# One core, one transformer layer: the value weights issued by SyncE, five warming products, another written-out order

## The chip, the cores and the metric

The kernel runs on one core of a Trainium2 chip. A core has five engines with a queue each: TensorE (PE in the profile; its weight loads are PEld), VectorE (DVE), ScalarE (ACT), GpSimd (POOL) and SyncE (SP), which here only issues DMAs. An engine takes its own queue strictly in order and waits on semaphores that the others raise. The metric is the device time of one execution in microseconds (us), before and after.

## The reference

`x` is 2048 x 448, in bf16. The layer is a linear attention with 16 heads of 28 columns, followed by a gated feed-forward of width 1792, each behind a layernorm and with a residual:

```python
qkv = (layernorm(x) @ wqkv) split into q, k, v of 16 heads
phi(q) = concat(softmax(q @ w_phi), softmax(-(q @ w_phi)))      # the same for k
kv = sum over s of phi(k)^T v ;  z = sum over s of phi(k)
o = (phi(q) @ kv) / (phi(q) . z + 1e-6)
h = x + o @ wo
h2 = h + (sigmoid(layernorm(h) @ w_gate) * (layernorm(h) @ w_up)) @ w_down
```

## The kernel before

**Tiles.** The 2048 rows are 16 tiles of 128 rows, numbered t = 0 to 15. Everything is a list of named tasks, one or a few instructions each, with an engine, a duration that the planner assumed, a latency (`lat`), dependencies and PSUM banks. `PLAN` (lines 30 to 71) writes out by number the order in which all tasks are put into the five queues; `planned()` (L113) reads it and `emit()` (L147) puts a semaphore wait ahead of a task where it needs one. A number followed by a point names the PSUM banks; a number followed by `~` puts the task on its other engine (`alt`). The durations and latencies in the text are what the planner worked with when it wrote the order: they issue nothing themselves.

**Start.** The q and k weights are multiplied with the per-head matrices `w_phi` first. `WT` (L431, PE) transposes a block of `wq` or `wk`, `mW` and `WTc` (L439, L446) centre it and copy it out, `PhiK` (L420, POOL) spreads `w_phi` into block diagonals, `fold` (L461, PE) multiplies, and `W2` (L469 on ACT, L472 on DVE) copies the product into `Wk2` or `Wq2`. The value weights `Wv` are centred only: `csum` (L477, PE) sums their columns, `csb` (L483, ACT) scales that and `Wvc` (L486, DVE) adds it. The first two tiles of x are transposed on PE (`xP`, L538, copied out by `xTc`, L544), the others by transposing DMAs (`xT0`, `xT1`, L349). `wm` (L413) are three products of constants into a bank nobody reads, which keep PE at work before data arrives; `dm` (L787) are spare products of the same kind which the plan places where it wants, five in all.

**Attention, keys and values.** For each pair of tiles: `kp` and `vp` (L500, PE) project, each in two halves, of which the second must follow the first. The statistics of x are `bst`, `agg` (L519, L521, DVE) and `ve`, `pow`, `neg` (L527 to L531, POOL). `ekp` and `ekm` (L572, ACT) are the two exponentials, `v1` (L577, ACT) the scaled values, `ss` and `rs` (L585, L588, DVE) sums and reciprocals, `phi` (L592, POOL at 1.7 us, or DVE at 1.1 us) the normalization, and `kv` (L605, PE) adds the tile's outer product to bank 4. There are three buffers each for the exponentials, `phi` and `v1`. DVE and POOL are kept from running large SBUF operations at once: a `phi` or `em` on DVE waits for the POOL task ahead of it in the plan, and the next POOL task waits for it (L126 to L133).

**Attention, queries.** `qp` (L500) projects, `eqp` and `eqm` (L627, ACT) exponentiate, `hs` (L641, POOL), `sq` (L637, L644, DVE), `rq0` (L646, DVE), `rq` (L648, POOL) and `em` (L654, POOL or DVE) normalize, and `eT` (L662) is a transposing DMA. When `kv` of tile 15 is done, `kvz` (L669, DVE) takes the sum out of PSUM. Then, by tile: `num` (L678, PE), `rd` and `o` (L686, L688, DVE), a transpose of o (`oP`, L696 on PE, for tiles 0 and 1; the DMA `oT`, L709, for pairs from tile 2), `wo_` (L723, L500), the residual `h` and its statistics `bst2`, `agg2` (L728, L745, L747), `ve2`, `pow2`, `nb` (L748 to L761, POOL), the normalized `hn` (L757, L763), and its transpose `hT` (`hP`, L771 on PE and a copy for tiles 0 and 1; a DMA, L783, after that).

**Feed-forward.** The tiles go in five chunks of 2, 4, 4, 4 and 2. `gu` (L500 with `wg_sb` and `wu_sb`) makes gate and up products for one chunk, seven groups per chunk, once `hT` of all of its tiles is there; `tg` (L818, ACT) is the tanh, `hh` (L825, DVE) the product, `dn` (L844, PE) the down product, `fin` (L851, DVE) the residual, `st` (L853, SP) the store.

**Loads.** SP issues, in the plan's order, `wk0 wk1 phk x0 x2 xT0(2) xT1(2) x4 xT0(4) wo1 xT1(4) wq0 wq1 x8` and so on (`x4` is tiles 4 to 7 of x). The two loads of the value weights, `wv0` and `wv1`, 224 KB each, are issued by ACT, behind `actld` (L336), an exponential of one column of `warm` that loads the table. At the very end `emit()` makes SP wait for all 44 DMA semaphores, in the order of their rings (L191 to L193):

```python
            for k, n in rings.items():
                for i in range(min(n, nring[k])):
                    wait("sp", ring_sems[k][i], (k, i), 16 * ((nring[k] - 1 - i) // n + 1))
```

Of the kernel before, what the change touches and what calls it, by code (L numbers as in the profile page):

```python
# [10 lines left out]
P = 128  # L11
# [19 lines left out]
20 14 18 3 19 21 11 2 8 9 12 0 23 24 16 43 7 17 5 57.7-7 58 59 653.0-0 68.0-0 69 15 10 1 6 62.1-1 63 65.2-2 66  # L31
71.3-3 25 26 22 29 27 28 30 31 32 70 64 67 72 73 116 118 4 654.0-0 655.0-0 163.4-4 164 60 61 165.5-5 89.6-6 92.7-7
86.0-0 95.1-1 93 96 90 87 166 91 88 117 119 94~ 120 121 122 97~ 656.2-2 110.2-2 111 125 123 113 126 124 112 132 130
134 136 131 135 133 137 167.3-5 127 128 44 129 114 138 33 46 34 35 36 37 38 39 40 41 45 42 47 139 168 172 185.6-7
179 171 186 187.0-1 169.2-3 188 170 178 189 190 191 180 173 174 175 74.4-4 181 176 75 76 77.5-5 80.6-6 203.0-3
177.4-4 182 78 192 141 193 81 79 197 196 198 140 183 199 194 115 145 200 204 207 208 205.2-5 221.1-7 206 83.0-0 184
195 222 82 214 215 209 216 210 143 211 217 84 218 201 226 225 212 85 219 223.3-6 101.2-2 224 107.5-5 202 213 108 102
239.0-1 240 232 233 103 234 109 227 144 142 147 228 148 146 149 13 150 151 243 244 235 229 156 158 236 152 246 157
159 154 247 155 153 230 237 241.2-7 220 104.6-6 105 242 98.5-5 99 257.0-3 258 231 245 100 251 106 250 262 311.2-5
238 248~ 160 161 162 249 253 254 255 252 261 268 264 265 266 312 277.1-6 275.0-7 269 314 313 319 271 272 273 276 315  # L40
280 279 320 259.2-3 260 278 256 263 267 293.0-5 282 283 284 287 286 270 281 294 289 290 321 316 322 291 297 305 298
327.2-7 295.1-3 288 304 274 328 337 296 299 285 330 306 336 345.0-6 362.1-5 346 329 363 292 355 354 347 372 348 371
364 323 317 324 300 307 301 308 318 302~ 303 309~ 310 51 49 55 56 48 50 52 326 325 54 447 338 331 339 356 379.3-7
453.2-2 380 448.6-6 511.4-4 454 332 455 340 449 333 657.0-0 456.0-0 349 357 450 350 430.2-5 341 334 358 351 342 335
359 352 382 457 389 381 365 512 513 451.0-0 452 431 507.6-6 508 440 388 514 344 343 360~ 535 353~ 536 361 509 529
413.1-3 396.0-7 461.4-4 414 433 432 510 439 423 366 530 367 537 531 368 462 538 539.2-2 532 458.6-6 463 459 533.5-5
460 397 369 373 374 370 375 540 534 416 415 422 693.2-4 694.5-6 695 696 697 699 376 377 465.1-1 468.3-3 698 383 390
700 469 466 470 701.2-4 702.5-6 703 704 406 405 399 398 707 705 464 53 515.3-7 516 384 467 385 391 708 706 392 549
541 709.0-1 710.5-6 711 712 713 715 717.2-4 718.3-7 719 720 378 714 550 542 475.0-0 472.1-1 716 543 721 723 471
517.5-6 518 722 473 551 476 474 477 557 565 724 386 387 393 394 400 544 545 546 552 407 553 554 395 725.2-4 726.0-1  # L50
727 728 733.5-6 734.3-7 735 736 558 547 729 731 555 559 730 732 566 560 561 562 741.2-4 742.0-1 743 744 739 737 563
478 548 567 740 738 745 747 568 569 570 519.3-7 401 746 748 482.5-5 479.6-6 752.2-2 520 483 480 481 402 408 424 417
425 484 426 418 403 571 556 564 572 755.0-1 756.4-6 757 758 404 409 427 410 573 581 441 411 753 582 574 583 584 585
434 761 759 762 760 435 763.3-5 764.2-7 765 766 767 769 771.4-6 772.0-1 773 774 768 442 419 420 770 777 775 428~ 778
# [11 lines left out]
938 888.3-3 885.5-5 889 886 879.2-2 880 946 882.4-4 944 883 644 751 652 890 959.3-5 960.0-2 961 962 963 965 966 964
967.1-6 968.4-7 969 970 973 971 975.0-2 976.3-5 977 978 972 974 981 979 982 980 983.1-6 984.4-7 985 986 987 989 988
990 991.3-5 992.0-2 993 994 999.1-6 1000.4-7 1001 1002 997 995 996 998 1007.3-5 1008.0-2 1009 1010 1003 1005 1004
1013 1014 1006 1023.1-1 956.6-6 957 1011 950.0-0 1012 951 953.2-2 1027.4-4 1024 954 881 822 884 952 955 887 958
1019.7-7 947.6-6 948 949 1028 1029 1025 1026 1020 1021 1022 1030 1015.3-3 1016 1017 1018  # L70
# [8 lines left out]
class _Graph:  # L79
# [33 lines left out]
    def planned(self):  # L113
# [3 lines left out]
        for item in PLAN.split():  # L117
# [29 lines left out]
    def emit(self, rings):  # L147
# [4 lines left out]
        with ExitStack() as es:  # L152
# [56 lines left out]
def build(nc, A_x, A_wqkv, A_w_phi, A_wo, B_w_gate, B_w_up, B_w_down, out):  # L209
# [16 lines left out]
    with ExitStack() as es:  # L226
# [667 lines left out]
```

## Time and profile before

| | us |
|---|---|
| runs of before | 206.13, 207.4, 208.04 (median 207.4) |
| the profiled execution: its time | 207.14 |
| the profiled execution: its span | 205.4 |
| PE busy | 196.1 (95%) |
| DVE busy | 131.2 (64%) |
| ACT busy | 97.5 (47%) |
| POOL busy | 77.2 (38%) |
| DMA, mean of the core's 16 engines | 103 GB/s |

The span is from the first to the last instruction; the execution's own time is 1.7 us longer. Times in the traces count from the span's start. PE's share is of modelled ends of pipelined products, so that 95% doesn't mean that it works at its best rate. The second part of the page shows the span in 40 slices of 5.1 us, in tenths:

```profile
PE   5999999997989799999999999999999999999994
DVE  2699999896979797886654387553664324352213
ACT  3869999999996461232531003374245130242000
POOL 8459997976787754803600002310003000000000
DMA  4999999219499973430565700054001200100022
```

Four engines are full in the first eight slices, the keys and values; from slice 16 on PE alone is.

### The profile page before, as it was taken

The numbers are of one execution on the slowest core, as the hardware profiler recorded it, in microseconds if no ns is written. First come the engines' busy times: TensorE is split into PE (matmuls) and PEld (weight loads), VectorE is DVE, ScalarE is ACT, GpSimd is POOL, SyncE is SP. The second block draws the span as 40 slices with busy tenths as digits, with TensorE's granted clock in tenths as the row PEclk, the third lists the DMA queues.
The fourth block names the chain that finished last, engine by engine and source line by source line (L and its number), as shares of the span: only waits on it lengthen the run. The fifth ranks groups of instructions, "written<-read, shape, count | busy, mean of one in ns | idle before, by whom it ended". The sixth has DMA issues, their size and how long they took to land.

```text
span 205.4 us, 5009 instructions
## 1 busy us (share of the span) xinstructions
PE 196.1 (95%) x2032; PEld 108.0 (53%) x2033; DVE 131.2 (64%) x304; ACT 97.5 (47%) x186; POOL 77.2 (38%) x139
## 2 busy tenths in 40 slices
PE   5999999997989799999999999999999999999994
PEld 2544544453456584555555554444444445786573
DVE  2699999896979797886654387553664324352213
ACT  3869999999996461232531003374245130242000
POOL 8459997976787754803600002310003000000000
PEclk9999999999999999999999999999999999999999
DMA  4999999219499973430565700054001200100022
GB/s 121 302 259 166 263 385 379 110 36 159 80 151 203 172 104 54 95 61 0 105 127 110 117 0 0 4 124 80 0 0 27 50 13 15 66 3 0 22 70 67
DMA packets 49751, 21.06 MB, mean 103 GB/s; under 512 B 40768, under 2 KB 48704, under 8 KB 49728
## 3 DMA queue, kind: packets, MB, share of 16 engines
q1 hardware_dynamic: 49184, 20.28, 44.9%
q10 hardware_dynamic: 544, 0.46, 0.8%
q8 instruction: 16, 0.26, 0.5%
q14 instruction: 7, 0.06, 0.1%
HBM read 9.20 MB, written 1.84 MB: 54 GB/s over the span
## 4 chain that ended last, share of the span: by engine, by line
PE 85%; DVE 5%; POOL 4%; DMA 2%; issue 1%; SPq 1%; ACT 0%; DVEq 0%; POOLq 0%
PE ps L500 58%; PE ps L844 21%; DMA x_sb<-in_A_x_dram 2%; PE ps L605 2%; POOL hh L592 2%; PE ps L678 1%; POOL halves L641 1%; POOL eq L654 1%; DVE sq L644 1%; DVE o_pad L688 1%; PE ps L461 1%; SPq L344 1%; DVE eq L654 1%; DVE hh L592 1%; PE ps L431 1%
## 5 line engine op out<-in xcount | busy, mean ns | idle before, releaser
L500 PE MATMUL ps<-xT,wg_sb 64*128 64x512 bf16 (+1 forms) x490 | 86.7, 333 | 0.5 <-DVE o_pad L688 0.5
L500 PE MATMUL ps<-xT,wu_sb 64*128 64x512 bf16 (+1 forms) x490 | 86.6, 333 | 0.0
L818 ACT ACTIVATE tg<-ps 128x512 f32<-128x512 f32 (+1 forms) x70 | 33.8, 511 | 73.0 <-PE ps L500 72.4
L825 DVE SCALAR_TENSOR_TENSOR hh<-tg,ps 128x512 bf16<-128x512 f32 (+1 forms) x70 | 38.1, 571 | 31.7 <-ACT tg L818 31.7
L500 PEld LDWEIGHTS ps<-xT,wg_sb 64*128 64x128 bf16 x490 | 45.7, 94 | 21.9 <-issue 1.5
L500 PEld LDWEIGHTS ps<-xT,wu_sb 64*128 64x128 bf16 x490 | 45.6, 94 | 15.3
L844 PE MATMUL ps<-wd_sb,hh 128*128 128x448 bf16 (+1 forms) x252 | 43.4, 332 | 0.0
L844 PEld LDWEIGHTS ps<-wd_sb,hh 128*128 128x128 bf16 x252 | 24.1, 98 | 17.6 <-issue 0.6
L851 DVE SCALAR_TENSOR_TENSOR x_sb<-ps,x_sb 128x448 bf16<-128x448 f32 (+1 forms) x18 | 10.0, 569 | 22.2 <-PE ps L844 22.2
L748 POOL TENSOR_SCALAR rs<-mv 128x1 f32<-128x1 f32 x14 | 2.7, 190 | 54.4 <-DVE mv L747 54.1
L592 POOL TENSOR_TENSOR hh<-hh,rsum 128x896 bf16<-128x896 bf16 x13 | 21.7, 1697 | 0.0
L572 ACT ACTIVATE hh<-ps,rs 128x448 bf16<-128x448 f32 x32 | 18.5, 647 | 1.7 <-PE ps L500 1.6
L627 ACT ACTIVATE eq<-ps,rs 128x448 bf16<-128x448 f32 x32 | 18.5, 675 | 0.5 <-PE ps L500 0.4
L585 DVE TENSOR_REDUCE ssum<-hh 128x32 f32<-128x896 bf16 x16 | 16.9, 1061 | 1.1 <-ACT hh L572 1.1
L641 POOL TENSOR_TENSOR halves<-eq 128x448 f32<-128x448 bf16 x14 | 13.5, 978 | 7.2 <-DVE sq L644 3.4
L500 PE MATMUL ps<-Wk,xT 64*128 64x448 bf16 x112 | 13.2, 351 | 0.5
L763 ACT ACTIVATE hn<-x_sb,nb,rs 128x512 bf16<-128x512 bf16 x11 | 8.9, 809 | 9.2 <-DMA xT<-hn 6.3
L500 PE MATMUL ps<-Wq,xT 64*128 64x448 bf16 x112 | 12.7, 351 | 0.0
L500 PE MATMUL ps<-Wvc,xT 64*128 64x448 bf16 x112 | 12.6, 350 | 0.1
L500 PE MATMUL ps<-wo_sb,oT 64*128 64x448 bf16 x98 | 11.2, 350 | 1.2 <-DVE o_pad L688 1.1
L654 POOL TENSOR_TENSOR eq<-eq,rq 128x448 bf16<-128x448 bf16 x12 | 11.2, 939 | 0.4
L577 ACT ACTIVATE hh<-ps,rs 128x448 bf16<-128x448 f32 x16 | 10.1, 661 | 0.5 <-PE ps L500 0.4
(100 smaller groups left out, 186.1 us busy)
## 6 DMA issues: line engine op xcount, KB each, us to landing
wu_sb<-in_B_w_up_dram SPq DMA_DIRECT2D x2, 896.0 KB, 9.6
wg_sb<-in_B_w_gate_dram SPq DMA_DIRECT2D x2, 896.0 KB, 10.9
out_dram<-x_sb SPq DMA_DIRECT2D x14, 112.0 KB, 1.9
x_sb<-in_A_x_dram SPq DMA_DIRECT2D x3, 448.0 KB, 5.2
wd_sb<-in_B_w_down_dram SPq DMA_DIRECT2D x3, 448.0 KB, 5.0
hh<-in_A_wqkv_dram SPq DMA_DIRECT2D x4, 196.0 KB, 3.1
wo_sb<-in_A_wo_dram SPq DMA_DIRECT2D x2, 336.0 KB, 7.5
x_sb<-in_A_x_dram SPq DMA_DIRECT2D x2, 224.0 KB, 5.2
```

Source lines behind the costliest of these rows:

```text
L500: r = e.matmul(ap(), lhsT=st(blk, rows), rhs=mv(blk, rows), start=first and i == 0, stop=not first and i == 2, tile_position=(rows.start, 0))
L572: task((key, t), "act", 0.53, lambda e, t=t, s=s, i=i, b=kb: e.activation(signs(ek[:, s, :])[:, :, :, i, :], heads2(bank[b()][:, 0:D]), AC ...
L577: return e.activation(v1[:, t % NV, :, 0:DH], bank[b()][:, 0:D].rearrange("p (h d) -> p h d", d=DH), ACT.Copy, scale=rs1[:, 0, t:t + 1])
L585: task(("ss", t), "dve", 1.0, lambda e, s=s: e.tensor_reduce(ssum[:, s, :], ek[:, s, :].rearrange("p (h d) -> p h d", d=DH), AX.X, ALU.add ...
L592: return e.tensor_tensor(phi[:, t % NPHI, :, 0:GP].rearrange("p k (a d) -> p k a d", d=DH), ek[:, s, :].rearrange("p (k a d) -> p k a d", ...
L627: task((key, t), "act", 0.53, lambda e, w=w, t=t, i=i, b=bk[j]: e.activation(signs4(eq[:, w, :, 0:GP])[:, :, :, i, :], heads2(bank[b()][:, ...
L641: task(("hs", t), "pool", 0.9, lambda e, w=w, half_=half_, by4=by4: e.tensor_tensor(half_, by4(eq[:, w, :, 0:GP])[:, :, :, 0:DH // 2], by4 ...
L654: return e.tensor_tensor(ap, ap, rq[:, w, :].rearrange("p (k h) -> p k h", h=2)[:, :, :, None].to_broadcast([P, NPAIR, 2, DH]), ALU.mult)
L818: task(("tg", c, f_), "act", 0.51 if n == 4 else 0.3, lambda e, j=j, N=N, b=gb[i]: e.activation(tg[:, j % NSG, 0:N], bank[b()][:, 0:N], AC ...
L825: e.scalar_tensor_tensor(hhT[c % 2][:, f_, 0:N], tg[:, j % NSG, 0:N], 1.0, bank[b()][:, 0:N], op0=ALU.add, op1=ALU.mult), deps)
L844: r = e.matmul(bank[b][:, cols], lhsT=hhT[c % 2][:, f_, ts], rhs=wd_sb[:, f_, cols], start=(f_ == 0), stop=(f_ == FT - 1))
L851: e.scalar_tensor_tensor(X(t)[:, cols], bank[got(first)[0]][:, cols], 0.5, X(t)[:, cols], op0=ALU.mult, op1=ALU.add), [nm, ("hn", t)])
```

## The change

It moves the value weights' loads from ACT to SP, after the transposes of tiles 2 and 3, and `x4` ahead of those transposes; makes five warming products instead of three; puts `warm` first of DVE's memsets; makes SP's last waits follow the order in which the DMAs were issued; and changes latencies and sizes that the planner assumes (loads 2.3 or 2.8, the transposes 2.8, `eT` 3.0, 2.2, 1.6 or 1.2 instead of 1.3 or 1.0, `oT` 2.0 or 1.3 instead of 0.95, `hT` 1.9 or 1.2 instead of 1.7 or 1.0). `PhiK` gets DVE as an alternative, which the new plan doesn't use. `PLAN` is another order of the same tasks, with two `wm` more and fifteen `dm` in the place of five.

```diff
-            if t.lock and t.alt and t.eng == "dve" and t.name[0] in ("phi", "em"):
+            if t.lock and t.alt and t.eng == "dve" and t.name[0] in ("phi", "em", "PhiK"):
...
-            for k, n in rings.items():
-                for i in range(min(n, nring[k])):
-                    wait("sp", ring_sems[k][i], (k, i), 16 * ((nring[k] - 1 - i) // n + 1))
+            last = {}
+            for t in done:
+                if t.kind is not None:
+                    sem, key, val, _ = ticket[t.name]
+                    last.pop(key, None)
+                    last[key] = (sem, val)
+            for key, (sem, val) in last.items():
+                wait("sp", sem, key, val)
...
-        task("onesU0", "dve", 0.12, lambda e: e.memset(onesU[LO, :], 0.0))
-        task("onesU1", "dve", 0.12, lambda e: e.memset(onesU[UP, :], 1.0))
+        task("onesU0", "dve", 0.12, lambda e: e.memset(onesU[LO, :], 0.0), behind=["warm"])
+        task("onesU1", "dve", 0.12, lambda e: e.memset(onesU[UP, :], 1.0), behind=["warm"])
...
-        LAST["act"] = "actld"
-        load("wv0", Wv[:, 0:2, :], wv_v[0:256, :].rearrange("(b p) n -> p b n", p=P), 0.3, "act")
-        load("wv1", Wv[:, 2:4, :], wv_v[192:448, :].rearrange("(b p) n -> p b n", p=P), 0.3, "act")
         load_x(2, 4)
+        load_x(4, 8)
         load_xT(2, 4)
-        load_x(4, 8)
+        load("wv0", Wv[:, 0:2, :], wv_v[0:256, :].rearrange("(b p) n -> p b n", p=P), 0.6)
+        load("wv1", Wv[:, 2:4, :], wv_v[192:448, :].rearrange("(b p) n -> p b n", p=P), 0.6)
         load_xT(4, 8)
...
-        NWARM = 3
+        NWARM = 5
```

Read by task number, the two plans order the work around the points that matter like this (PE; `gu0` is the first chunk, its groups numbered by 2; `,0` and `,1` are first and second halves):

```
before  wm x3, dm, WT of k x4, dm x2, xP0, xP1, fold of k x8, dm, csum, kp0, kp1, vp1, vp0, ...
after   wm x5, dm, WT of k x4, fold, xP0, fold x2, xP1, fold x5, dm x7, kp0, csum, kp1, dm, kp2,0, ...

before  kv13 kv14 kv15 qp4,0 num1 qp4,1 num0 wx1 dm oP1 qp7,0 wo_1 oP0 qp7,1 wx0 wo_0 qp6,0 qp5,0
        num3 qp6,1 hP1 num2 hP0 qp5,1 gu0,0 num4 num5 gu0,2 wo_(2,3) gu0,4 gu0,6 num7 num6 wo_(4,5) gu0,8 ...
after   qp4,0 kv13 kv14 kv15 qp4,1 num0 qp3,0 num1 qp3,1 oP0 wx0 wx1 oP1 wo_0 qp6,0 wo_1 qp6,1 dm x3
        hP0 num2 dm hP1 dm dm num3 gu0,0 gu0,2 num5 num4 gu0,4 qp5,0 wo_(2,3),0 qp5,1 wo_(2,3),1 gu0,6
        num6 num7 gu0,8 wo_(4,5) gu0,10 qp7,0 gu0,12 qp7,1 ...
```

On POOL, `z_eq` (L307) and `v1one` (L306) go behind `PhiK`, `pow4` behind `phi0`, and `rq1 rq0 em0 em1` ahead of `phi13` instead of behind it. On DVE, `Wvc` goes behind `ss0`; `WTc` of one block of q and `v1` of tile 9 come over from ACT; two of `em` go to POOL, and `hn` of two tiles instead of three is DVE's. `eT0` is issued ahead of `eT1`.

More of the change, by code (lines that the diff above doesn't have):

```diff
@@ L66 @@
[L66 to L70, printed above, removed]
+0 4 18 8 9 3 23 24 25 26 27 28 29 30 31 32 33 34 35 36 37 44 38 39 40 47 43 10 41 14 16 42 19 20 21 1 2 17 7 11 12
@@ L342, in load @@
             behind, LAST[eng] = [LAST[eng]] if LAST.get(eng) else (), name
-            lat = 1.3 if name in ("wk0", "wk1", "phk", ("x", 0), "wv0") else 1.7 if name in ("wv1", ("x", 2)) else 2.3
+            lat = 1.3 if name in ("wk0", "wk1", "phk", ("x", 0)) else 1.7 if name in (("x", 2), ("x", 4)) else 2.3 if name[0] == "w" else 2.8
             task(name, eng, 0.5, lambda e: e.dma_start(dst, src), list(deps), lat=lat,
@@ L419, in build, with f @@
             bs = slice(2 * i, 2 * i + 2)
-            task(("PhiK", i), "pool", 0.54, lambda e, bs=bs: e.tensor_tensor(
-                PhiK[:, bs, :, :], wphK[:, bs, None, :].to_broadcast([GP, 2, HL, DH]),
-                maskK[:][:, None, :, None].to_broadcast([GP, 2, HL, DH]), ALU.mult), ["phk", "maskK"])
+            def f(e, bs=bs):
+                return e.tensor_tensor(PhiK[:, bs, :, :], wphK[:, bs, None, :].to_broadcast([GP, 2, HL, DH]),
+                                       maskK[:][:, None, :, None].to_broadcast([GP, 2, HL, DH]), ALU.mult)
+            task(("PhiK", i), "pool", 0.54, f, ["phk", "maskK"], alt=("dve", 0.34, f), lock=True)
         WLOAD = [["w%s%d" % (n, i) for i in range(2)] for n in "qk"]
@@ L664, in build @@
                     in_=eq[:, w:w + n, :, :].rearrange("p t k s -> p (t k s)")),
-                    [("em", t) for t in range(a, a + n)], lat=1.3 if a < 6 else 1.0, kind="tr", size=1.42 * n)
+                    [("em", t) for t in range(a, a + n)], lat=3.0 if a < 2 else 2.2 if a < 6 else 1.6 if a < 10 else 1.2, kind="tr", size=1.42 * n)
         Q_OF = {t: ("qp", t // 2, 1) for t in range(NT)}
@@ L783, in build @@
                 task(("hT", t), "sp", 1.25, lambda e, t=t: e.dma_start_transpose(
-                    out=hnT[:, :, TS(t)], in_=hn[:, t % NHN, :]), [("hn", t)] + read, lat=1.7 if t < 6 else 1.0, kind="tr", size=0.72)
+                    out=hnT[:, :, TS(t)], in_=hn[:, t % NHN, :]), [("hn", t)] + read, lat=1.9 if t < 6 else 1.2, kind="tr", size=0.72)
         for i in range(40):
```

87 lines of the change are left out of this document (46 added, 41 removed).

## The prediction

> **What bounds the kernel now.** I read the busy times by stretch first, cut where the work changes: keys and values, the seam (from `kvz` to the first `gu`), the first chunk of the feed-forward, the rest.
>
> ```profile
> 10.00:47.60 37.60, 36.77 (x442) 18.27 (x441) 35.55 (x77) 35.37 (x68) 30.99 (x35) 1.00 0.89 226
> 47.60:60.10 12.50, 10.79 (x118) 5.05 (x116) 10.73 (x30) 11.57 (x23) 10.37 (x16) 1.00 0.61 133
> 60.10:81.25 21.15, 19.89 (x301) 13.94 (x301) 16.75 (x47) 10.88 (x25) 12.77 (x25) 1.00 0.82 136
> 81.25:202.60 121.35, 121.33 (x1128) 66.46 (x1126) 63.05 (x130) 33.96 (x63) 16.87 (x43) 1.00 0.23 48
> ```
>
> Columns: stretch and length, then PE, PEld, DVE, ACT, POOL busy (x: instructions), PE's clock, DMA share, GB/s. From 81.25 on PE never stops: nothing can be won there, and each product that an earlier stage leaves over is paid in full. In the first stretch PE, DVE, ACT and POOL are all nearly full, so each must be walked. PE idles 1.7 us in the seam and 1.3 in the first chunk. Next, the chain of waits and the timeline, for who starts these stretches:
>
> ```profile
> 2.23 4.83 DMA x_sb<-in_A_x_dram
> ...
> 47.73 0.64 DVE kvz L669
> ```
> ```profile
> 2.27 1.46 PE L413 MATMUL ps<-warm 128*128 128x512 bf16 x3 [2.27 <-DVE warm L301]
> ...
> 6.59 1.07 POOL L420 TENSOR_TENSOR PhiK<-wphK,maskK 112x224 bf16<-112x224 bf16 x2 [1.79 <-DMA wphK<-in_A_w_phi_dram]
> ...
> 10.10 3.30 PE L500 MATMUL ps<-Wk,xT 64*128 64x448 bf16 x28
> ```
>
> The first line is from the chain of waits: start, length, what. PE's first product waits for `warm`; the first x tiles land at 2.23 + 4.83 = 7.06, `phk` at 6.5, where POOL's wait ends; `fold`, `W2` and `kp0` (10.10) hang on both. The seam, on SP, PE and DVE:
>
> ```profile
> 44.13 2.64 SPq L662 DMA_TRANSPOSE eqT<-eq  x2
> ```
> ```profile
> 49.62 0.39 PE L678 MATMUL ps<-kvz,eqT 112*128 112x58 bf16 x8 [1.07 <-DVE sq L644]
> ...
> 60.11 0.27 PE L500 MATMUL ps<-xT,wg_sb 64*128 64x256 bf16 x1 [0.46 <-DVE o_pad L688]
> ```
> ```profile
> 48.38 0.62 DVE L644 TENSOR_REDUCE sq<-halves 128x32 f32<-128x448 f32 x1
> 50.05 0.26 DVE L686 RECIPROCAL rden<-ps 128x16 f32<-128x16 f32 x1 [1.05 <-PE ps L678]
> ```
>
> `num1` starts at 49.62, though `kvz` ended at 48.37 and the named `sq` isn't its input. The view of `eqT` gives 3.2, 4.5 and 5.4 us from issue to landing (least, median, most). `eT1`, issued at 44.13, is the slow one: 44.13 + 5.4 = 49.5. A DMA was last, and DVE lost 1.05 us. The packet records show why: a 16 KB packet of the instruction queue at 47.70, and almost no transpose packets from 47.6 to 48.9. In the first chunk one wait stands out:
>
> ```profile
> PEld ps L500 <- DMA oT<-o_pad: 1.4, 2, 1.2
> ```
>
> It is `wo_` of tiles 4 and 5, which waits 1.2 us for its transpose.
>
> **The start.** The edits of the start meet at `kp0`. With `warm` first of DVE's memsets PE begins at 0.86 + 0.48 and a hop, 1.4; five `wm` and a `dm` at the 0.43 of the first ones end at 4.0, and `WT` can't start before 4.06: they cost nothing there. Without ACT's two loads beside it, x0 lands between 2.75 us after issue (as `wk1`: issued 1.25, used from 4.06) and 4.83 as now: 5.0 to 7.06; I take 5.5, nearer to `wk1`, since only x, `phk` and the weights ahead are left in the queues. `phk` (issued 1.74, 4.8 now) likewise 4.5 to 6.5, taken as 5.2; `PhiK` then ends at 6.4 instead of 7.67. `WT` still waits for `wk1`, and ACT's four `WTc` end at 7.14 as now; the last folds come at 7.3 to 7.9, the copies `W2` at 9.2, seven `dm` of 0.22 at 9.4. So `kp0` starts at 9.4; early end 9.2, late end 10.4 (folds end at 8.9 as now, plus 1.5 of `dm`). `z_eq` (1.59) and `v1one` (0.30) behind `PhiK` fall into POOL's waits. `csum` (1.0) now lies on PE between `kp0` and `kp1`; it needs `wv1`, issued by SP at about 7.4 and, by `wq1`'s 3.5 to today's 5.4 us, there at 10.9 to 12.8, against 11.0 when PE is ready: 0 to 1.8 us of waiting, taken as 0. SP pays 0.45 + 0.49 for the two issues; `wo1` (0.60), queued ahead of `xT1(4)`, leaves, so that lands 0.3 later, at 13.1; its user `kp2` comes at 13.7.
>
> **Keys and values.** POOL sets the pace through `phi`. From `kp0`: 1.57 for its products, 0.2, two exponentials 1.16, `ss0` 1.1, the two `Wvc` now behind it 1.04, `rs0` with its hop 0.43: `phi0` starts at 14.9 instead of 16.03. Behind it POOL has `pow4` more (1.1) and, ahead of `phi13`, two `rq` and two `em` more (2.15), `maskP` less (0.15): `phi13` ends at 42.85 - 1.1 + 1.1 + 2.15 - 0.15 = 44.85. By the rule of the two engines `phi14` on DVE waits for it, at 44.9 where it now starts at 45.13 behind `rs15`, so `kvz` comes 0.2 earlier, at 47.5. DVE gets 1.1 us more (`WTc` 0.52, `v1` 0.57) but starts 1.5 earlier. **Term 1: -0.2** (+0.7 with the late `kp0`; -0.4 with the early one). Behind the waiting `phi14` stand `phi15` and `kvz` on DVE, and PE's `kv14` and `kv15` wait for them: nothing hides it.
>
> **The seam.** `em0` ends at 42.2 and `em1` at 43.1, so `eT0` and `eT1` are issued 1 to 2 us earlier and land by 3.4 to 5.4 us at 45.6 to 49.5: `num0` waits for `kvz` alone, and `num1` has a `qp` half ahead of it. From `kvz` on, DVE's order is the chain: `kvz` 0.64, four `sq` 2.4, two `rd` 0.44, four `rq0` 0.88, two `o` 1.22, two each of `bst2`, `agg2`, `em`, `ve2` 1.26, 0.34, 1.2, 0.3. That is 8.7; eleven neighbours overlap by 0.08, and 0.5 of hops come back: 8.3. Then `pow2` on POOL 0.8, `hn` 0.33, `hP`, `hT` and hops 1.25: 10.7 us, where it now takes 60.11 - 47.73 = 12.4. **Term 2: -1.7** (0 to -2.2), and `gu0` starts at 58.2. The six `dm` there (1.3) lie in PE's waits for `hn`; with that cover gone, they would be paid. **Term 3: +2.7.** `qp5` and `qp7` are no longer done when `gu0` starts. Two such pairs (28 products) take 2.75 us in the chain at 44.15, 2.65 from start to start.
>
> **The first chunk.** `wo_` of tiles 4, 5 ended at 71.98. Now, from 58.2: five `gu` groups of 1.53, four `num` and mode changes 1.6, `qp5` and `wo_(2,3)` 2.65, `wo_(4,5)` 1.6 give 71.7, while its transpose can start sooner (`em7` about 1 us earlier, `eT6` is ahead of it on SP): landing near 69, needed at 70. **Term 4: -1.2**, the wait (0 if it comes back). `hT5`, on which the second chunk starts, landed at 81.1 and PE came at 81.25; it follows `wo_(4,5)` by 9.1 us, 80.8 at the latest, when PE comes at 80.8.
>
> **The end.** The 44 last waits run as 22 instructions, 0.06 us apart from 203.41. The records show one pause of 0.3 for the last store, landed at 204.57, and seven more instructions behind it. In the new order that store is last; the walk takes 22 x 0.06 = 1.35 without a pause, 204.76, instead of 205.02. **Term 5: -0.25.** Latencies, sizes, `behind` and `PhiK`'s alternative issue nothing: 0. In the rest `dn11` between `gu` groups adds two mode changes of 0.1 to 0.2, and `em`, `hn` move between engines that idle half of the time there: 0.
>
> Sum: -0.2 - 1.7 + 2.7 - 1.2 - 0.25 = -0.65. On the profiled execution's 207.14 (span 205.4 and 1.7 around it) that is 206.5; its time is 0.3 below the median of the runs, 207.4.
>
> **Rivals.** (a) *The seam gives nothing* (slower). Its place is the relay between DVE and POOL: both `em` on DVE wait for `rq4` on POOL, `pow2` on POOL waits for both `em`, and `hn` for that. If `rq4`, 54.4 now and 53.9 by my walk, isn't earlier, `gu0` stays at 60.1, and the moved `qp` are paid: 207.14 + 2.7 - 1.2 - 0.25 = 208.4. It decides from `gu0` later than 58.9 on. With the `oT` wait kept as well: 209.6. For it: POOL is 83% busy in the seam. Against: `hs6` now stands ahead of `pow2` and leaves. (b) *Everything that starts earlier is kept* (faster). If POOL's own gaps in the first stretch (one of 1.3, where it waits for `phi8` on DVE) close, so that `phi13` keeps the 1.1 that `phi0` gains and the early `kp0`'s 0.2, `kvz` comes 1.3 earlier; with term 2 at -2.2 the sum is -1.3 - 2.2 + 2.7 - 1.2 - 0.25 = -2.25 and the time 204.9. For it: DVE, ACT and POOL idle 2.1, 2.2 and 6.6 us in the first stretch. Against: `phi13` has 2.15 us more ahead of it, and DVE 1.1 more work. (c) *The seven `dm` run slowly.* The first products start 0.40 to 0.43 apart, later ones 0.22; the folds reach full speed at 8.3, 6.0 us after the first product, although the clock's column says 1.00 throughout. With `warm` first, PE starts at 1.4, so full speed by the same span is at 7.4. If it isn't there at 7.9, the seven cost 1.5 more, `kp0` comes at 10.9 and the time is 207.9. The Trainium skill (TensorE: Matmul & The Clock Gate, "What's actually happening") says that PE gets its full clock after one busy window of some 3.4 us, and that the windows run freely. By that rule full speed comes between 4.8 and 8.2, so it leaves (c) a small chance; the trace agrees, its 6.0 lying between 3.4 and 6.8.
>
> **Numbers.** Forecast 0.43 (205.6 to 207.4 alone), (a) 0.25, (b) 0.24, (c) 0.08. About 1% (2.1 us) can be told from no change: faster is below 205.3, slower above 209.5. (b) lies below in most of its cases, 0.20, and the forecast's early end reaches it with 0.04: 0.24. Slower is the worse half of (a), where the `oT` wait or `csum`'s 1.8 joins it, 0.13, and (c) with a waiting `csum`, 0.02: 0.15. The rest, 0.61, is the same. The range, 204.0 to 208.9, takes in (b) to 0.9 below its price and (a) to 0.5 above.
>
> **What would show it.** In the changed profile: PE's first product at 1.4; x0's landing under 3.5 us; `kp0` at 9.4; `phi0` at 14.9; `kvz` at 47.5; `num0` right behind `kvz`, without the 1.05 on DVE; the first `gu` near 58.2; no wait for `oT`; the second chunk at 80.7. I am wrong if the first `gu` comes after 58.9, if PE has a new wait behind 81, or if `phi13` doesn't end near 44.9.

## The result and the profile after

The changed kernel takes 208.24 us (median of 20 runs) against 206.41 us (20 runs of the kernel before beside it): 1.009 times as long, 95% interval 1.0071 to 1.0109. The forecast was 206.5, no change. The profiled execution after has a span of 206.8 us where the one before had 205.4.

First the busy times by stretch of the changed kernel, cut at the same events as before (`kvz`, the first `gu`, the second chunk, the last products); columns as before:

```profile
10.00:48.75 38.75, 36.79 (x438) 17.81 (x436) 35.12 (x77) 34.30 (x65) 30.49 (x34) 1.00 0.90 245
48.75:60.07 11.32, 9.97 (x99) 4.39 (x96) 10.36 (x26) 9.47 (x19) 9.13 (x14) 1.00 0.49 93
60.07:82.49 22.42, 22.27 (x329) 15.71 (x331) 20.06 (x56) 13.26 (x29) 15.83 (x30) 1.00 0.59 111
82.49:204.25 121.76, 121.74 (x1128) 64.52 (x1124) 60.53 (x121) 34.96 (x64) 16.96 (x41) 1.00 0.23 47
```

`kvz` comes 1.0 later (48.75 for 47.73), the seam is 1.1 shorter (11.32 for 12.4), the first chunk 1.3 longer (22.42 for 21.15); what follows is 0.4 longer up to the last `fin` (121.76 for 121.35) and 0.3 shorter behind it. The first `gu` starts at 60.07, where it started at 60.11. So the products that the new plan leaves for the first chunk are paid in full, and nothing in front of them was gained to pay for them.

The start went as forecast, but for the load `x0`, which landed at 6.02, 3.8 us after its issue, where under 3.5 was forecast; that cost nothing, since `xP0` now stands behind the first `fold`. From the timeline of PE and POOL after:

```profile
1.51 2.31 PE L419 MATMUL ps<-warm 128*128 128x512 bf16 x5 [1.51 <-DVE warm L308]
...
4.85 1.08 POOL L427 TENSOR_TENSOR PhiK<-wphK,maskK 112x224 bf16<-112x224 bf16 x2 [0.87 <-DMA wphK<-in_A_w_phi_dram]
...
9.38 1.74 PE L507 MATMUL ps<-Wk,xT 64*128 64x448 bf16 x14
```

`kp0` starts at 9.38, `phi0` at 14.86. What went wrong stands further on in the timelines of DVE and then POOL:

```profile
23.21 1.08 DVE L592 TENSOR_REDUCE ssum<-hh 128x32 f32<-128x896 bf16 x1
25.88 0.63 DVE L526 BATCH_NORM_STATS2 st<-x_sb 128x6 f32<-128x448 bf16 x1 [1.58 <-DMA x_sb<-in_A_x_dram]
26.42 0.34 DVE L595 RECIPROCAL rsum<-ssum 128x32 f32<-128x32 f32 x1
```
```profile
24.96 1.04 POOL L536 TENSOR_TENSOR rs<-rs,neghalf 128x4 f32<-128x4 f32 x1
26.84 1.70 POOL L599 TENSOR_TENSOR hh<-hh,rsum 128x896 bf16<-128x896 bf16 x1 [0.84 <-PE ps L468]
```

The new plan puts `bst14` on DVE ahead of `rs5`. `bst14` reads the load `x12`, which lands at 25.85; DVE stands still for 1.58 us with `rs5` behind it, and POOL for 0.84 us, since `phi5` needs `rs5` (the table names PE's `ps`, which `phi5` doesn't read). In the kernel before `bst14` came at 27.53, behind `rs5`; its DVE:

```profile
23.95 0.35 DVE L588 RECIPROCAL rsum<-ssum 128x32 f32<-128x32 f32 x1
...
27.53 1.09 DVE L519 BATCH_NORM_STATS2 st<-x_sb 128x6 f32<-128x448 bf16 x2
```

Another 0.26 is lost at 41.8, where POOL waits for `rq0` of tile 1. `phi13` ends at 46.02 instead of the forecast 44.85, and `kvz` follows. In the seam, DVE and POOL:

```profile
56.93 0.41 DVE L764 TENSOR_SCALAR hn<-x_sb,mv,rs 128x512 bf16<-128x512 bf16 x1
57.79 1.05 DVE L764 TENSOR_SCALAR hn<-x_sb,mv,rs 128x512 bf16<-128x512 bf16 x1 [0.45 <-POOL rs L757]
```
```profile
57.73 1.94 POOL L648 TENSOR_TENSOR halves<-eq 128x448 f32<-128x448 bf16 x2
```

`hn1` takes 1.05 us where `hn0` takes 0.41: POOL's `hs6` starts 0.06 us before it. The wait for the transpose of `wo_(4,5)`, 1.2 us before, is gone from the waits of PE's weight loads; 0.4 us is left, once:

```profile
PEld ps L507 <- DMA oT<-o_pad: 0.4, 1, 0.4
```

### The profile page after: what moved, and what is told of

Read it like the earlier page. It is cut to its first block, busy times and chain, and to the rows that moved or that the text cites. A ratio compares the mean times of both kernels' runs of the same rounds, so it can differ in the third digit from the quotient of the medians.

```text
span 206.8 us, 5032 instructions
## 1 busy us (share of the span) xinstructions
PE 198.8 (96%) x2045; PEld 106.9 (52%) x2045; DVE 132.4 (64%) x303; ACT 97.5 (47%) x185; POOL 79.4 (38%) x141
## 4 chain that ended last, share of the span: by engine, by line
PE 76%; POOL 7%; SPq 5%; DVE 5%; issue 2%; DMA 2%; ACT 2%; POOLq 0%; DVEq 0%; ACTq 0%
PE ps L507 51%; PE ps L851 21%; SPq L356 3%; SPq L351 2%; DMA hh<-in_A_wqkv_dram 2%; POOL eq L661 2%; PE ps L685 2%; ACT hh L579 2%; POOL hh L599 2%; POOL halves L648 2%; DVE sq L644 1%; POOL rs L757 1%; PE ps L612 1%; DVE hh L599 1%; POOL rq L655 1%
## 5 line engine op out<-in xcount | busy, mean ns | idle before, releaser
L858 DVE SCALAR_TENSOR_TENSOR x_sb<-ps,x_sb 128x448 bf16<-128x448 f32 (+1 forms) x18 | 10.1, 569 | 22.0 <-PE ps L851 22.0
L579 ACT ACTIVATE hh<-ps,rs 128x448 bf16<-128x448 f32 x32 | 18.4, 650 | 4.1 <-PE ps L507 2.1
L661 POOL TENSOR_TENSOR eq<-eq,rq 128x448 bf16<-128x448 bf16 x14 | 13.1, 942 | 0.6
L507 PE MATMUL ps<-Wvc,xT 64*128 64x448 bf16 x112 | 13.1, 350 | 0.2
L749 DVE TENSOR_TENSOR x_sb<-ps,x_sb 128x448 bf16<-128x448 f32 x14 | 8.3, 616 | 3.7 <-PE ps L507 3.6
L770 ACT ACTIVATE hn<-x_sb,nb,rs 128x512 bf16<-128x512 bf16 x12 | 9.5, 813 | 2.3 <-POOL nb L768 2.2
## 6 DMA issues: line engine op xcount, KB each, us to landing
wd_sb<-in_B_w_down_dram SPq DMA_DIRECT2D x3, 448.0 KB, 10.3
```

Of the source, the lines that this page charges most:

```text
L507: r = e.matmul(ap(), lhsT=st(blk, rows), rhs=mv(blk, rows), start=first and i == 0, stop=not first and i == 2, tile_position=(rows.start, 0))
L579: task((key, t), "act", 0.53, lambda e, t=t, s=s, i=i, b=kb: e.activation(signs(ek[:, s, :])[:, :, :, i, :], heads2(bank[b()][:, 0:D]), AC ...
L661: return e.tensor_tensor(ap, ap, rq[:, w, :].rearrange("p (k h) -> p k h", h=2)[:, :, :, None].to_broadcast([P, NPAIR, 2, DH]), ALU.mult)
L770: task(("hn", t), "act", 0.56, lambda e, t=t, hnv=hnv: e.activation(hnv(), windows(X(t)), ACT.Identity, bias=nb[:, t:t + 1], scale=rs2[:, ...
L858: e.scalar_tensor_tensor(X(t)[:, cols], bank[got(first)[0]][:, cols], 0.5, X(t)[:, cols], op0=ALU.mult, op1=ALU.add), [nm, ("hn", t)])
```

## The experiments

Theory A: the loss is in these two places, the landing that the plan puts in front of POOL's chain (about 0.8 to 1.0 us) and `hs6` beside `hn1` (0.6). All kernels start from the changed one unless said otherwise. Edits of the order are shown with task names in the place of the plan's numbers.

**bst14 later.**

```diff
 (DVE)
-ss5 bst14 rs5 ss6 bst12
+ss5 rs5 ss6 bst14 bst12
```

> One move in the changed kernel: on DVE the statistics of x tile 14 (bst14, which needs the load of x rows 12 to 15, landed at 25.85 us) go behind the sums ss6 instead of ahead of the reciprocal rs5. Theory A (the planned order put a landing ahead of POOL's chain): DVE's idle 1.58 us ahead of bst14 goes, phi5 on POOL starts at 26.0 instead of 26.84, phi13 ends near 45.1 instead of 46.02, kvz starts near 47.8 instead of 48.75, the first gate product near 59.2 instead of 60.07; ratio to the kernel before near 1.005 instead of 1.009. Rival B (the seam has its own clock and takes up any gain): kvz near 47.8, first gate product still near 60.0, ratio 1.009. Rival C (POOL's gap at phi5 is the wait for ps that the table of waits names, not rs5): kvz stays at 48.7, ratio 1.009.

Measured: 1.0054 (1.0021 to 1.0086). `rs5` at 24.76, `phi5` at 26.40 without a gap, `kvz` at 48.29, first gate product at 59.60, second chunk at 82.01: the first gate product moved with `kvz`, so B and C fall. The ratio alone wouldn't tell, since a second copy of the changed kernel, below, has 1.0061. The gain in this trace is half of what A said, for a reason of A's own kind: in this execution `wq1` landed at 15.69 instead of 15.25, DVE's `mW` steps wait for products of it ahead of `rs1`, and POOL lost 0.38 us at `phi1`:

```profile
16.55 1.03 POOL L536 TENSOR_TENSOR rs<-rs,neghalf 128x4 f32<-128x4 f32 x1
17.96 1.70 POOL L599 TENSOR_TENSOR hh<-hh,rsum 128x896 bf16<-128x896 bf16 x1 [0.38 <-DVE rsum L595]
```

**The same from the other side: x12 earlier.**

```diff
-        load_xT(12, 16)
         load_x(12, 16)
+        load_xT(12, 16)
```

> One move in the changed kernel: SP issues the load of x rows 12 to 15 ahead of the two transposes of x^T's last chunk instead of behind them, some 4 us sooner; DVE's order stays. Theory A (the late landing, not DVE's order as such, is what DVE waits for ahead of rs5): x12 lands near 22, bst14 starts behind ss5 without a gap at 24.2, phi5 follows pow8 at 26.0, kvz near 47.8, first gate product near 59.2, ratio near 1.005. The two transposes land some 0.6 us later (near 21.0 and 23.2), which their products, far behind, have room for. Rival C (POOL's gap at phi5 has another cause): kvz stays near 48.7 and the ratio near 1.009.

> The changed kernel once more, to stand beside the three others on the same chip: ratio 1.007 to 1.011. Its profile is read for the landing of the load x12, for which theory A expects that phi13's end and kvz follow it from run to run: the first look had it at 25.85 us with kvz at 48.75.

Measured: 1.0072 (1.0041 to 1.0104), and the unchanged copy beside it 1.0061 (1.0032 to 1.0090). DVE's and then POOL's timeline with the early load:

```profile
23.03 1.08 DVE L592 TENSOR_REDUCE ssum<-hh 128x32 f32<-128x896 bf16 x1 [0.28 <-ACT hh L579]
24.04 0.62 DVE L526 BATCH_NORM_STATS2 st<-x_sb 128x6 f32<-128x448 bf16 x1
```
```profile
25.88 1.70 POOL L599 TENSOR_TENSOR hh<-hh,rsum 128x896 bf16<-128x896 bf16 x1
```

`x12` lands at 20.39. No gap, `kvz` at 47.79, first gate product at 59.10, second chunk at 81.53: in the trace all of A's figures. The median hardly shows it (207.93 beside 208.03). One reason is that the landing scatters: `x12` lands at 25.85 and 25.51 in two profiles of the changed kernel, at 24.51 and 26.32 in two kernels that left the loads alone, and `kvz` follows it, so the stall is 0 to 1 us, not 1 us. Another is that three of the twelve runs with the early load are of a long kind that comes below, and one of the twelve of the copy.

**hs6 behind hn1.**

```diff
-[("eqp", t), ("eqm", t), opt(("sq", t - 2)) if t > 3 else None]
+[("eqp", t), ("eqm", t), opt(("sq", t - 2)) if t > 3 else None, ("hn", 1) if t == 6 else None]
```

> One added dependence in the changed kernel: hs6 on POOL starts only when hn1 on DVE is done. Theory A (hn1 took 1.05 us because hs6 ran on POOL beside it): hn1 takes 0.4 us, the copy hT1 ends near 59.3 instead of 59.92, the first gate product starts at 59.4 to 59.5 instead of 60.07, ratio to the kernel before near 1.006; hs6 starts about 0.5 us later, which costs nothing if its successors have that much room. Rival B (hn1 is slow for a reason of its own): hn1 stays near 1.05 us, the first gate product stays near 60.07 and the ratio near 1.009.

Measured: 1.0035 (1.0005 to 1.0066). `hn1` on DVE:

```profile
58.73 0.41 DVE L764 TENSOR_SCALAR hn<-x_sb,mv,rs 128x512 bf16<-128x512 bf16 x1 [0.45 <-POOL rs L757]
```

0.41 us, and from `kvz` to the first gate product 10.66 us instead of 11.32 (49.70 to 60.36). `kvz` itself is 0.95 later than in the changed kernel's profile, for a reason that comes below. In the kernel before the two also met, with DVE first (the line has `hn1` and `hn0`): there `hn` kept its time, 0.32 and 0.41, and POOL's `hs7` took 1.11 us instead of 0.97.

```profile
57.75 0.64 DVE L757 TENSOR_SCALAR hn<-x_sb,mv,rs 128x512 bf16<-128x512 bf16 x2
```
```profile
58.11 1.11 POOL L641 TENSOR_TENSOR halves<-eq 128x448 f32<-128x448 bf16 x1
```

The Trainium skill (SBUF — State Buffer, "SBUF: two separate sides") says that GpSimd and a VectorE operation in a two-port mode lock each other out for a whole instruction, whoever starts first. The traces agree in kind: `hn1`, begun 0.06 us after `hs6`, ended at 58.84, just behind it (two `hs` end at 59.67, the first near 58.7), though a full block would have put all of its own 0.41 after that. Whether `hn` runs in such a mode no trace shows.

**em5 and em4 behind hn.**

```diff
 (DVE)
-bst2_0 agg2_0 em5 em4 ve2_0 bst2_1 agg2_1 ve2_1 hn0 hn1
+bst2_0 agg2_0 ve2_0 bst2_1 agg2_1 ve2_1 hn0 hn1 em5 em4
 (PE; rd and o of tiles 5 and 4 likewise on DVE)
-gu0,2 num5 num4 gu0,4
+gu0,2 gu0,4 num5 num4
```

> The changed kernel with em5 and em4 moved on DVE behind hn1, so that the statistics of the second hidden tile no longer stand behind them; num5, num4 and their four DVE steps move behind the third block of gate products, since eT4 is later by as much. Theory A (a relay of em5 and em4 on DVE sets the first gate product): bst2 of tile 1 starts near 55.6 instead of 55.97 and bst2 of tile 0 is followed at once by ve2 of tile 0, pow2 of tile 0 starts near 54.9 instead of 56.13, hn1 ends near 57.8 instead of 58.84, the first gate product starts at 58.7 to 59.0 instead of 60.07; ratio 1.003 to 1.005. Rival B (wo_1, ended at 55.51, and what follows it set it): first gate product no earlier than 59.5, ratio 1.007 or more. Either way em4 ends near 58.9, eT4 lands near 63.2, and a stall of PE at num5 would show that the time only moved.

Measured: 1.0116 (1.0071 to 1.0160). The two stretches:

```profile
48.00:58.35 10.35, 9.82 (x98) 4.39 (x98) 8.78 (x24) 9.47 (x19) 7.22 (x13) 1.00 0.26 51
58.35:82.47 24.12, 23.07 (x329) 15.45 (x331) 21.15 (x58) 13.27 (x29) 17.62 (x32) 1.00 0.75 125
```

The first gate product came at 58.35, 1.7 earlier, and the second chunk where it was, at 82.47. Of the 1.7, 0.75 is `kvz`: in this execution `x12` landed at 24.5, so `kvz` came at 48.00, and `phi5` without a gap: A's stall is absent where the landing is early. Of the seam's 0.97, 0.65 is `hn1` at 0.41 us again, since `hs6` waits for `em4` here and starts only at 58.34; the relay of `em5` and `em4` itself is worth 0.3. Nothing of the gain was kept: `eT4` was issued 2.2 us later and landed at 63.6, 5.4 us after its issue instead of 4.3, and the first chunk waited.

**The three moves together.** `bst14` behind `ss6`, `rs1` ahead of `mW`, `hs6` behind `hn1`; run twice.

```diff
 (DVE)
-ss1 mW03 mW01 ss2 rs1
+ss1 rs1 mW03 mW01 ss2
```

> Three small moves in the changed kernel together: bst14 behind ss6 on DVE, the reciprocal rs1 ahead of the two steps mW that wait for the products of the late load wq1, and hs6 on POOL behind hn1. Theory A (the planned landings cost 0.8 to 1.0 us at kvz, and hs6 beside hn1 0.55 to 0.65 us): they add up, kvz near 47.7, first gate product near 58.6 to 58.7, second chunk near 81.1, ratio 1.000 to 1.002, which is the 1.4 to 1.6 us that the sum of the forecast missed. Rival B (what is gained at the seam waits later in the first chunk of gate products): the first gate product near 58.7, the second chunk no earlier than 82.0, ratio 1.005 or more.

> The three small moves (bst14 behind ss6, rs1 ahead of the mW steps, hs6 behind hn1) once more, beside the two others: first gate product at 58.4 to 58.8, second chunk at 80.8 to 81.2, ratio to the kernel before 1.001 to 1.005.

Measured: 1.0037 (1.0005 to 1.0068) and 1.0056 (1.0027 to 1.0085); medians 207.10 and 207.07. The first of them:

```profile
47.83:58.50 10.67, 9.97 (x98) 4.38 (x96) 9.38 (x26) 9.47 (x19) 8.28 (x14) 1.00 0.49 92
58.50:80.93 22.43, 22.28 (x329) 15.70 (x331) 20.34 (x56) 13.27 (x29) 16.66 (x31) 1.00 0.62 114
```

`kvz` 47.83, seam 10.67, first chunk 22.43, second chunk at 80.93, span 205.2: this is the timeline that the prediction wrote for the changed kernel (47.5, 10.7, 22.5, 80.7). The times add up as A said, but the ratio is not A's 1.000 to 1.002: the kernel is slower than before by 0.4 to 0.6%. So the kernel before is better than its profile, which the next two runs look at.

**The kernel before, twice more.**

> The kernel before, unchanged, for a second profile of it. Theory D: the seam's gain of 1.7 us was read off a profile in which eT1 landed late (5.4 us after its issue, beside a 16 KB packet of instructions), and other executions of the kernel before do not have it: eT1 lands within 3.5 us, num0 starts right behind kvz, the first gate product near 59, span near 204.4 instead of 205.4. Rival E: the late landing belongs to this kernel's place of the packet, eT1 takes over 5 us again, the first gate product is near 60 and the span near 205.4.

> The kernel before, unchanged, for a third profile of it: the same two theories, D (eT1 within 3.5 us, the first gate product near 59, span near 204.4) and E (eT1 over 5 us, the first gate product near 60, span near 205.4).

Measured: 1.0003 and 1.0012, spans 204.7 and 204.2. In the first, by stretch, and by the tile that `eT` writes:

```profile
10.00:47.47 37.47, 36.71 (x443) 18.25 (x441) 35.27 (x77) 35.31 (x68) 30.91 (x34) 1.00 0.82 226
47.47:59.04 11.57, 10.81 (x116) 4.94 (x114) 10.74 (x30) 11.38 (x22) 10.16 (x16) 1.00 0.65 137
59.04:80.48 21.44, 19.99 (x300) 13.93 (x301) 17.15 (x48) 10.89 (x25) 13.20 (x26) 1.00 0.81 134
```
```profile
L678 PE MATMUL ps<-kvz,eqT x128: 187/190/201, 48.2 to 117.7; 112*128 112x58 bf16 x128
```

The first `num` starts at 48.2, right behind `kvz` (48.12), instead of 49.6; `eT1` took 3.2 us, not 5.4, in both. The first gate product is at 59.04 and 58.99, not 60.11, and the seam 11.57 and 11.39 long, not 12.4. D holds: about 0.9 of the 12.4 us of seam that the prediction set out to shorten was one execution's late transpose. The 1.2 us at `wo_(4,5)` is in both of them, so that term's base was sound. The prediction named a 16 KB packet of instructions at 47.70 as the reason why `eT1` was late. The same packet stands at 47.81 and 47.94 in these two executions, while `eT0` is under way, and `eT0` landed after 3.3 us in both. So the packet alone isn't the reason; why the two transposes were late once stays open.

**The last waits alone, in the kernel before.** Edit: the lines of `emit()` as in the change.

> The kernel before with one part of the change: the waits at the program's end in the order in which the queues' last transfers are issued. Theory: the waits of the earlier rings cost nothing any more after the last store's, some five waits of 0.05 us, 0.25 us less: ratio 0.9988, which five rounds can hardly tell from 1. Rival: the time after the last store's landing is not made of these waits, ratio 1.000.

Measured: 0.9986 (0.9957 to 1.0015). The interval holds 1, so the times can't tell it from none. The traces can: from the end of the last `fin` to the span's end it is 2.41 us in three profiles of the kernel before, 2.15 here and 2.15 in the changed one.

**Filling PE's empty stretch.** Four of the twelve runs of the three moves, both times, stood 1.4 us or more above the lowest; so did six of twenty of the changed kernel, and 22 of 92 in all with its copy and the variants of `bst14`, `x12` and `hs6`. The profile with `hs6` behind `hn1` was of such a run. PE there:

```profile
6.52 0.35 PE L468 MATMUL ps<-PhiK,hh 112*128 112x112 bf16 x2 [0.40 <-ACT hh L453]
...
7.89 1.14 PE L468 MATMUL ps<-PhiK,hh 112*128 112x112 bf16 x10
8.82 1.48 PE L794 MATMUL ps<-warm 128*128 128x512 bf16 x3
10.49 0.81 PE L794 MATMUL ps<-warm 128*128 128x512 bf16 x3 [0.18 <-DVE st L526]
11.23 1.74 PE L507 MATMUL ps<-Wk,xT 64*128 64x448 bf16 x14
```

and in the changed kernel's own profile:

```profile
7.08 0.86 PE L468 MATMUL ps<-PhiK,hh 112*128 112x112 bf16 x10
7.78 1.68 PE L794 MATMUL ps<-warm 128*128 128x512 bf16 x7
9.38 1.74 PE L507 MATMUL ps<-Wk,xT 64*128 64x448 bf16 x14
```

The same dummies start 0.43 us apart until about 10.3 in the one and 0.22 apart from 7.8 in the other (x7 in 1.68 us); `kp0` comes 1.85 later, 1.67 counted from the first `fold`, and what hangs on it too. The clock's column says 1.00 in both. Just before the first `fold` PE has nothing to do for 0.4 us in both (up to 6.52 and 6.34); in the kernel before two dummies stood in such a place.

```diff
-WT10 WT11 WT13 WT12 fold100
+WT10 WT11 WT13 WT12 dm30 fold100
```

> The three small moves, and one dummy product more on PE in the empty stretch between the transposed weights (last at 5.34) and the first fold (6.34). If the executions that run some 1.8 us longer come from that empty stretch, which keeps PE's products at half rate until 10.4 us in them: none of the twelve runs stands 1.4 us or more above the lowest, where four of twelve did with the three moves alone, and the mean ratio falls by 0.002 to 0.003. Rival (the instant of the full rate depends on something outside the kernel): the same share of long runs, two to five of twelve.

> The changed kernel with one dummy product in PE's empty stretch ahead of the first fold, and nothing else. Theory F (the empty stretch lets PE's products stay at half rate in part of the executions): no run 1.4 us or more above the lowest but for the scatter of x12's landing, highest run below 208.8, median 207.5 to 207.8, ratio 1.005 to 1.007. Rival: long runs near 209.3 as in the changed kernel, median 208.0 to 208.3, ratio 1.007 to 1.010.

```diff
 (the kernel before)
-WT12 WT10 WT11 WT13 dm1 dm2 xP0
+WT12 WT10 WT11 WT13 xP0
```

> The kernel before without the two dummy products that stand between the transposed weights and the first transposes of x, so that PE has an empty stretch of about 0.9 us there. Theory F: a larger share of long executions than the kernel before has beside it, a second group of times 1 to 2 us above the first, ratio 1.002 to 1.008. Rival: the times stay as they are, ratio 0.999 to 1.001.

Measured: with the three moves 1.0040 (1.0026 to 1.0053), ten runs from 206.92 to 207.55, none long, where 8 of 24 were without the dummy. PE there:

```profile
5.76 0.45 PE L794 MATMUL ps<-warm 128*128 128x512 bf16 x1
...
7.81 1.68 PE L794 MATMUL ps<-warm 128*128 128x512 bf16 x7
```

In the changed kernel alone 1.0070 (1.0055 to 1.0086), six runs from 207.77 to 208.07, none long; but in its copy only one of twelve was, so six say little. The kernel before without its two dummies has 1.0056 (1.0029 to 1.0084), its nine runs anywhere from 204.93 to 209.10. F holds for the three moves and agrees with the other two; its figure for the median of the changed kernel (207.5 to 207.8) was a little low. An empty stretch doesn't always bring the late case, though. Without the two dummies the profiled execution is the lowest one, and its PE is at full rate right behind a stretch of 0.97 us (it also waits only 0.2 us for `oT`):

```profile
6.96 0.62 PE L538 MATMUL ps<-ident,x_sb 128*128 128x128 bf16 x8 [0.97 <-DMA x_sb<-in_A_x_dram]
```

Nor does the late case belong to the changed kernel. 29 of 139 runs of the kernel before, taken beside these, stood 1.4 us or more above the lowest of their group, and the profile with the last waits was of such a run (208.03). It has both dummies, but `x0` landed at 7.63 instead of 6.7 to 7.1, PE stood empty for 0.86 us, and its products ran at half rate until 11.5:

```profile
7.68 1.03 PE L543 MATMUL ps<-ident,x_sb 128*128 128x128 bf16 x8 [0.86 <-DMA x_sb<-in_A_x_dram]
...
10.42 0.95 PE L482 MATMUL ps<-hh,ones 128*128 128x448 bf16 x2
...
11.88 1.36 PE L505 MATMUL ps<-Wk,xT 64*128 64x448 bf16 x10
```

So the late case makes the runs of both kernels scatter, in similar shares, and it isn't shown to be part of the difference between them. The Trainium skill (TensorE: Matmul & The Clock Gate, "What's actually happening") says that the full clock comes after one busy window of some 3.4 us and that windows run freely, so that the instant differs from run to run. The traces agree that it differs: full rate comes from 4.3 us in the copy of the changed kernel, by 6.3 in its first profile and at about 10.3 in the profile with `hs6` behind `hn1`. They don't bear out the length: the first product is at 1.51 in all three, so full rate comes after 2.8 us in the one and 8.8 in the other.

**Other orders.** Four kernels try to win back more by another order up to the second chunk, found by small moves against a walk of the queues.

> The same instructions as the changed kernel (and hs6 behind hn1), in another order up to the second chunk of gate products, found by trying small moves against a walk of the queues with durations of the changed kernel's trace; loads keep their order on SP. That walk has kvz 2.2 us and the second chunk 3.8 us earlier than in the changed kernel. If the queues up to the seam are what the change lost in, as theory A has it: second chunk at 78.5 to 80.0, ratio 0.990 to 0.998. If landings scatter as they do between runs and an order this tight meets them, as a rival: second chunk at 81 or later, ratio 1.003 or more.

> The changed kernel with hs6 behind hn1 and another order of the compute engines' instructions up to the second chunk of gate products; SP's order is left exactly as it was, loads and transposes alike. A walk of the queues with the changed kernel's durations has kvz at 46.2 and the second chunk 3.5 us earlier than in the changed kernel. Theory A (the loss lies in the order of DVE and POOL up to the seam): kvz at 46.2 to 47.2, first gate product at 56.6 to 57.6, second chunk at 78.6 to 80.0, ratio to the kernel before 0.990 to 0.996. Rival (the walk leaves out what the chip adds): second chunk at 81 or later, ratio 1.000 or more.

> As the reordered kernel, with one more condition: qp5 stands ahead of the first gate product, as it did in the kernel before, where the changed kernel had put it behind. Theory A with the deferral itself harmless (1.3 us of products cost PE the same on either side of the seam, as long as PE would be idle ahead of it): ratio within 0.003 of the other reordered kernel. Rival (the deferral is what cost the time): 1.3 us better, ratio 0.006 below the other's. Rival (qp5's four exponentials and two banks ahead of the seam hold up the first chunk): ratio 0.005 or more above.

> The three small moves, and qp5 back ahead of the first gate product in PE's idle time there, with the order behind the seam adapted (from the kv's end to the second chunk, SP's order untouched). If the deferral of qp5 is a plain loss of PE time once PE idles ahead of the seam: the first gate product no later than 58.0, the second chunk 0.8 to 1.3 us earlier than in the three moves alone, near 80.0, ratio 0.997 to 1.000. Rival (the exponentials and banks of qp5 and later transposes take it back, as in the two reordered kernels): second chunk at 81 or later, ratio 1.003 or more.

```diff
 (the last of the four, PE around the seam)
-wo_0 qp6,0 wo_1 qp6,1 dm x3 hP0 num2 dm hP1 dm dm num3 gu0,0
+wo_0 wo_1 qp6,0 qp6,1 qp5,0 hP0 num2 hP1 qp5,1 gu0,0 num3
```

Measured, in this order: 1.0201 (1.0152 to 1.0250), 1.0135 (1.0104 to 1.0166), 1.0118 (1.0079 to 1.0158), 1.0081 (1.0052 to 1.0111). All misses. Contrary to the words of its expectation, the first also moved late weight loads on SP, one of them (`wd0`) from 26.2 to 59.97, ahead of the first chunk's transposes. The second has PE at half rate until 10.8 (`kp0` at 11.37), which the walk doesn't know. The last is the clearest, by stretch:

```profile
47.88:57.45 9.57, 9.30 (x98) 4.34 (x97) 8.67 (x24) 9.32 (x19) 8.03 (x13) 1.00 0.28 55
57.45:81.13 23.68, 21.63 (x322) 14.70 (x324) 20.80 (x56) 13.68 (x29) 16.27 (x30) 1.00 0.77 124
```

With `qp5` back in front the first gate product comes at 57.45, 1.05 earlier than with the three moves alone, and the second chunk at 81.13, 0.2 later. Seam and first chunk together take 33.25 us here, 33.1 with the three moves, 33.7 in the changed kernel, 34.5 with `em5` and `em4` moved, and 33.5, 33.0 and 32.5 in three profiles of the kernel before. What these orders take out of the first they put into the second. The third of the four, with `qp5` in front as well, has 32.6, but its `kvz` came at 48.78; its ratio is within 0.003 of the second's. So the deferral of `qp5` alone isn't the loss, and none of these orders is faster than the kernel before.

## Why the prediction was wrong

Two steps failed. The first is **Term 2, the seam, -1.7**. Between the two profiles it was -1.1; against what the kernel before usually does it was -0.1 to -0.3 (11.57 and 11.39 to 11.32). About 0.9 of it was never there to be won: the 12.4 us were read off an execution in which `eT1` took 5.4 us, and the text took that for the kernel's own wait. Another 0.65 was eaten by `hn1` beside `hs6`; the walk priced `hn` at 0.33, about as `hn1` stood in the trace of before, where DVE was first and POOL waited. The walk's length, 10.7, was right: 10.67 once `hs6` is out of the way.

The second is **Term 1, -0.2**, which between the two profiles was +1.0, the larger miss there. With `x12` landing at 24.5 it was +0.5 to +0.6 (`kvz` at 48.08 in the filled kernel, 47.47 and 47.60 before), and without any stall still +0.2 to +0.3 (47.79 with the early load). Its parts were right (`kp0` 9.38, `phi0` 14.86, POOL with new gaps in two places only), but the text walked POOL's queue and took DVE's for granted. The trace of before showed the landing of `x12`, 25.77, and the new plan showed `bst14` ahead of `rs5`. The base was late too: 47.73 is 0.1 to 0.3 behind the kernel before's other two profiles.

**Terms 3 and 4, +2.7 and -1.2**, hold: 22.42 for the first chunk against 21.15 and a forecast of 22.5, the wait for `oT` down to 0.4. **Term 5, -0.25**, holds in the traces; but between the second chunk and the last `fin` 0.4 us came on top (121.76 to 122.17), where the text put 0 for two mode changes. PE has the same 1126 products there in both kernels and never waits, but in the new order it changes between products of 64 and of 128 rows nine times instead of five: four more, about 0.1 us each.

**The rivals.** (a) came true by its price, 208.4, and by its condition (`gu0` after 58.9, `rq4` done at 54.8), but the relay that it named isn't the root: with the three moves `rq4` was done at 53.9, as the walk had it, and `gu0` came at 58.50, the relay untouched. (b) had nothing for it. (c) was given 0.08 and judged by one instant (its price by its own sum is 206.5 + 1.5 = 208.0, not 207.9). In fact the instant differs between runs: full rate came from 4.3 to 10.9 us with the first product at 1.51, where the text allowed 4.8 to 8.2, and the late case, 1.67 us, is in up to a third of the runs. A dummy where the plan took two away ends it with the three moves, which the text didn't price at all; but the kernel before has such runs as well. The range, to 208.9, held the time.

The sum in the end, filled kernel against the second profile of before, stretch by stretch: `kvz` +0.6, seam -0.3, first chunk +1.0, the rest +0.1 to +0.2: +1.4 to +1.5, its span 206.1 for 204.7; its ratio, 1.0070, is 1.4 us too. The 0.4 that the changed kernel's median has on top (0.1 in its copy) agrees with its late landings and late clock; how it splits between them wasn't measured. Of the chunk's +1.0 it stays open how much another order can win back: the four tried won nothing.

## What to carry to other kernels

Before a wait is counted as a gain, see it in a second execution: a transposing DMA that landed 2 us late once was half of a term here. In a plan written out by hand, look for every instruction that waits for a load, on every engine, and at what stands behind it: the reciprocals behind `bst14` and `mW` fed the queue that sets the pace. And a gain at a stage's start counts only when the next stage's own inputs come earlier too.

## What the runs showed of the hardware

- With PE's first product at 1.51, its products went from half to full rate (from 0.43 to 0.22 us apart at 512 columns) at 4.3 to 5.3 us, between 5.7 and 6.4, or at 10.1 to 10.9, while the clock's column said 1.00; the last case put `kp0` off by 1.67 us. With one dummy product of about 0.4 us in an empty stretch none of 16 runs was long, where 22 of 92 were without.
- A DVE `TENSOR_SCALAR` of 128 x 512 in bf16 took 1.05 us instead of 0.41 beside a POOL `TENSOR_TENSOR` that reads bf16 and writes f32, begun 0.06 us earlier; with DVE first, POOL's took 1.11 instead of 0.97.
- One load's landing, `x12`, scattered from 24.5 to 26.3 us over nine profiles with the same loads ahead of it, and the same transposing DMA took 3.2 or 5.4 us.
- Four more changes of PE between products of 64 and of 128 rows went with 0.4 us more for the same 1126 products.
